# Moving the load and the transpose of an FFN bias to later places in a fused attention and FFN kernel

## The chip, the cores and the metric

One core of one Trainium2 chip. The metric is the device time of one execution in microseconds (us). All runs are on a single core; each kernel was run several times, and beside each kernel the kernel before was run on the same chip. The granted clock is the share of TensorE's full clock that the chip allowed, as the trace records it.

## The reference, cut to what matters

```python
# x: (1, 2048, 512), 32 heads of 128, 2048 cached keys and values, FFN width 1792
xn = layernorm(x)
q = (xn @ wq) split into 32 heads
o = softmax(q k^T / sqrt(128)) v
s = concat(o) @ wo
h = relu(xn @ w1 + b1) ** 2          # b1 has 1792 values: 14 rows of 128
g = silu(h @ w2 + b2)
out = x + s * g
```

The change touches only how b1 reaches its place. The kernel computes h with the FFN channels on the 128 partitions, so it needs b1 as 14 columns of 128. It loads it as 14 rows of 128 (a dense load), turns the rows into columns by a transpose on TensorE, and copies the result from PSUM to SBUF as 32-bit values.

## The kernel before

It is hand-scheduled: every instruction is emitted in a chosen order. A helper records what each instruction depends on and emits the waits. The beginning is written out by hand. The first head's keys come as rows in two halves and are transposed on TensorE. The query rows are normalised in four tiles of 128; each is transposed, projected for head 0 (`first_proj`) and head 1 (`second_proj`), and scores, exponentials and weighted sums (`gen_scores`, `gen_pv`) start as soon as a tile is there. After that a loop over 1024 steps keeps TensorE full (busy for 1206.00 of 1206.00 us between 16 and 1222 us in the profile below); projections and FFN matmuls are "fill jobs" between the steps.

```python
    # on GpSimd, after the memsets at the start
    tok_b1 = S.emit_dma(GP, partial(_dma, out=b1b[:], in_=B_b1.rearrange("(c p) -> c p", p=P)),
                        sl_b1)
    ...
    def bias_rows():
        t_b1[0] = E(PE, partial(_peT, out=psA[:, 1536:1600].bitcast(BF16)[:, 0:NFC], in_=b1b[:],
                                ident=ident[0:NFC, 0:NFC]), deps=[tok_b1, t_ident])

    def bias_copy():
        t_b1[0] = E(DV, partial(_copy, out=b1f[:],
                                in_=psA[:, 1536:1600].bitcast(BF16)[:, 0:NFC]), deps=[t_b1[0]])
    ...
    # gen_scores, first head: the scores are written to psA, where the bias columns lie for a moment
                      deps=[t_k0[b], t_q0[qt], t_exp[pi - 2] if pi >= 2 else t_b1[0]],
    ...
    # the beginning, in program order (cut)
    k0_copy(1)
    ln_rstd(0, 1, eng=DV)
    first_copy(0)
    first_proj(0)
    bias_rows()
    ln_scale(0, 1)
    first_evac(0)
    bias_copy()
    first_transpose(1)
    gen_scores(0)
    ln_bn(0, 2)
    gen_scores(1)
    ...
    first_evac(3)
    second_proj(3)
    second_evac()
    t_bankF[:] = [t_q0[3], tok_xT[0][3]]
    gen_pv(3)
    gen_scores(6)
```

The softmax here doesn't subtract the row's maximum and nothing guards it: scores larger than these inputs give would overflow.

## Time and profile before

| What | Value |
|---|---|
| Device time, median of 3 runs | 1237.77 us (1237.75 to 1237.85) |
| Execution that was profiled | 1238.05 us, span 1236.3 us |
| TensorE busy | 1231.7 us of the span |
| First scores start | 7.96 us |

The span is counted inside the execution; the device time is some 1.8 us longer. The profiled execution was 0.3 us slower than the timed ones. "PE" is TensorE's matmuls, "PEld" its weight loads, which run beside the matmuls: they are busy for 818.8 us and the matmuls for 1231.7 of a span of 1236.3 us, so they overlap. In a timeline line the first number is the start in us from the beginning of the span, the second the time covered, and the brackets give the idle time before and what ended it.

### The profile page before, as it was taken

What the parts mean: (1) busy time and instruction counts of PE and PEld (TensorE: products, weight loads), DVE (VectorE), ACT (ScalarE), POOL (GpSimd) and SP (SyncE); (2) the same over time, 40 slices, a digit from 0 to 9 for tenths busy, and PEclk for the clock granted to TensorE, in tenths of its full rate; (3) what the DMA queues carried; (4) which work ended last, traced back from release to release, by engine and by line L of the source; (5) the groups of instructions that cost most, each with busy time, mean ns of one, the idle gap of its engine ahead of it and who ended that gap; (6) DMA issues with size and microseconds to landing.
All of it is one profiled execution on the core that took longest, in us unless ns stands there. A gap on an engine that the chain in (4) does not pass through costs nothing.

```text
span 1236.3 us, 26934 instructions
## 1 busy us (share of the span) xinstructions
PE 1231.7 (100%) x11885; PEld 818.8 (66%) x11885; DVE 472.8 (38%) x953; ACT 1053.5 (85%) x1044; POOL 31.9 (3%) x73
## 2 busy tenths in 40 slices
PE   9999999999999999999999999999999999999999
PEld 7666666666666666666666666666666666666665
DVE  4453323244435332334444532333344333324333
ACT  7888888888888888888888888888888888888885
POOL 1010000000002000000000200000000000000000
PEclk9999999999999999999999999999999999999999
DMA  9999998777879897778778878787788789878771
GB/s 211 203 231 209 185 178 134 130 144 143 139 152 172 141 161 129 139 139 145 133 133 170 172 138 143 141 148 134 133 146 148 146 154 158 137 134 146 145 123 31
DMA packets 686868, 185.41 MB, mean 150 GB/s; under 512 B 673536, under 2 KB 685568, under 8 KB 686752
## 3 DMA queue, kind: packets, MB, share of 16 engines
q1 hardware_dynamic: 684656, 179.62, 80.4%
q0 software_dynamic: 1424, 3.81, 1.2%
q8 instruction: 94, 1.54, 0.6%
q10 hardware_dynamic: 672, 0.26, 0.1%
q14 instruction: 22, 0.18, 0.1%
HBM read 96.60 MB, written 2.10 MB: 80 GB/s over the span
## 4 chain that ended last, share of the span: by engine, by line
PE 99%; DMA 0%; DVE 0%; issue 0%; SPq 0%; DVEq 0%
PE psO L157 38%; PE psA L152 36%; PE psF L152 25%; DMA kT<-in_A_k_cache_dram 0%; PE psA L157 0%; DVE out_t L165 0%; PE psF L196 0%; DVE tmp_t L175 0%; PE psO L196 0%; PE psO L152 0%; DVE xnT L179 0%; SPq L208 0%; PE psA L196 0%; DVEq L119 0%
## 5 line engine op out<-in xcount | busy, mean ns | idle before, releaser
L161 ACT ACTIVATE pT<-psA 128x1024 bf16<-128x1024 f32 x1024 | 1043.5, 1023 | 163.5 <-PE psA L152 118.1
L157 PEld LDWEIGHTS psO<-v_sb,pT 128*128 128x128 bf16 x8192 | 547.7, 98 | 240.5 <-issue 12.5
L157 PE MATMUL psO<-v_sb,pT 128*128 128x129 bf16 x8192 | 631.6, 220 | 0.0
L152 PE MATMUL psA<-qt_sb,kT 128*128 128x512 bf16 x2032 | 604.8, 379 | 0.0
L179 DVE COPY o_un<-psO 128x258 f32<-128x258 f32 x256 | 97.4, 422 | 399.4 <-PE psO L157 398.7
L152 PE MATMUL psF<-xnT,wq_sb 128*128 128x512 bf16 (+1 forms) x520 | 168.9, 374 | 0.2 <-DVE xnT L179 0.2
L152 PE MATMUL psF<-wo_all,oT 128*128 128x512 bf16 x480 | 163.8, 379 | 0.0
L152 PEld LDWEIGHTS psA<-qt_sb,kT 128*128 128x128 bf16 x2032 | 156.9, 98 | 0.0
L179 DVE CAST qt_sb<-psF 128x512 bf16<-128x512 f32 (+1 forms) x130 | 88.0, 677 | 97.4 <-PE psF L152 97.4
L165 DVE TENSOR_TENSOR o_bf<-o_un,rden 128x512 bf16<-128x512 f32 x128 | 88.6, 692 | 4.7 <-DVE rden L183 0.3
L152 PEld LDWEIGHTS psF<-xnT,wq_sb 128*128 128x128 bf16 x520 | 50.2, 98 | 60.1 <-issue 0.3
L171 DVE TENSOR_SCALAR r_t<-psF,b1f 128x512 bf16<-128x512 f32 x56 | 42.0, 750 | 117.5 <-PE psF L152 117.5
L152 PEld LDWEIGHTS psF<-wo_all,oT 128*128 128x128 bf16 x480 | 46.9, 98 | 56.4
L152 PE MATMUL psF<-xnT,w_sb 128*128 128x512 bf16 x224 | 77.1, 379 | 0.0
L152 PE MATMUL psF<-w_sb,h2T 128*128 128x512 bf16 x224 | 74.2, 379 | 0.0
L152 PEld LDWEIGHTS psF<-xnT,w_sb 128*128 128x128 bf16 x224 | 21.9, 98 | 26.5
L152 PEld LDWEIGHTS psF<-w_sb,h2T 128*128 128x128 bf16 x224 | 21.9, 98 | 26.5
L165 DVE TENSOR_TENSOR z_t<-psF,b2bc 128x512 f32<-128x512 f32 x16 | 11.1, 692 | 67.2 <-PE psF L152 67.2
L165 DVE TENSOR_TENSOR acc<-psF,acc 128x512 f32<-128x512 f32 x28 | 19.3, 689 | 29.9 <-PE psF L152 29.9
L208 POOL DMA_DIRECT2D out_dram<-out_t x12 | 6.7, 554 | 891.0 <-DVE out_t L165 891.0
L165 DVE TENSOR_TENSOR h2T<-r_t 128x512 bf16<-128x512 bf16 x56 | 23.8, 425 | 1.9
L183 DVE RECIPROCAL rden<-o_un 128x4 f32<-128x4 f32 x128 | 22.9, 179 | 4.4
(47 smaller groups left out, 165.6 us busy)
## 6 DMA issues: line engine op xcount, KB each, us to landing
v_sb<-in_A_v_cache_dram SPq DMA_DIRECT2D x127, 512.0 KB, 4.7
wq_sb<-in_A_wq_dram SPq DMA_DIRECT2D x127, 128.0 KB, 3.1
wo_all<-in_A_wo_dram SPq DMA_DIRECT2D x4, 1024.0 KB, 6.7
w_sb<-in_B_w_dram SPq DMA_DIRECT2D x14, 256.0 KB, 4.3
oT<-o_bf SPq DMA_TRANSPOSE x128, 4.0
x_t<-in_A_x_dram POOLq DMA_DIRECT2D x16, 128.0 KB, 3.4
kT<-in_A_k_cache_dram SPq DMA_TRANSPOSE x127, 4.5
x_ln<-in_A_x_dram SPq DMA_DIRECT2D x15, 128.0 KB, 3.8
```

The costliest lines, as they stand in the source:

```text
L152: return e.matmul(out, lhsT, rhs, start=start, stop=stop)
L157: return e.matmul(out, lhsT, rhs, start=start, stop=stop, skip_group_check=True)
L161: return e.activation(out, in_, func, bias=bias, scale=scale)
L165: return e.tensor_tensor(out, in0, in1, op)
L171: return e.tensor_scalar(out, in0, scalar1=scalar1, scalar2=scalar2, op0=op0, op1=op1)
L179: return e.tensor_copy(out, in_)
L183: return e.reciprocal(out, in_)
L208: return e.dma_start(out, in_)
```

## The change

Its intent: take the small load out of the first microseconds, in which the keys arrive (the DMA engines are busy for 0.56 of the first 5 us), take the transpose off the way to the first scores, and free the first scores from a wait on the bias. The whole diff:

```diff
-    tok_b1 = S.emit_dma(GP, partial(_dma, out=b1b[:], in_=B_b1.rearrange("(c p) -> c p", p=P)),
-                        sl_b1)
-
@@ bias_rows, bias_copy
-        t_b1[0] = E(PE, partial(_peT, out=psA[:, 1536:1600].bitcast(BF16)[:, 0:NFC], in_=b1b[:],
-                                ident=ident[0:NFC, 0:NFC]), deps=[tok_b1, t_ident])
+        t_b1[0] = E(PE, partial(_peT, out=bankF(1)[:, 0:64].bitcast(BF16)[:, 0:NFC], in_=b1b[:],
+                                ident=ident[0:NFC, 0:NFC]), deps=[tok_b1, t_ident, tok_xT[0][TPB - 1]])
-                                in_=psA[:, 1536:1600].bitcast(BF16)[:, 0:NFC]), deps=[t_b1[0]])
+                                in_=bankF(1)[:, 0:64].bitcast(BF16)[:, 0:NFC]), deps=[t_b1[0]])
@@ gen_scores
-                      deps=[t_k0[b], t_q0[qt], t_exp[pi - 2] if pi >= 2 else t_b1[0]],
+                      deps=[t_k0[b], t_q0[qt], t_exp[pi - 2] if pi >= 2 else None],
@@ fill jobs
-    bank_no = [1]
+    bank_no = [0]
@@ the beginning
     ln_rstd(0, 1, eng=DV)
+    tok_b1 = S.emit_dma(GP, partial(_dma, out=b1b[:], in_=B_b1.rearrange("(c p) -> c p", p=P)),
+                        sl_b1)
     first_copy(0)
     first_proj(0)
-    bias_rows()
     ln_scale(0, 1)
     first_evac(0)
-    bias_copy()
@@
     second_proj(3)
     second_evac()
-    t_bankF[:] = [t_q0[3], tok_xT[0][3]]
+    bias_rows()
+    bias_copy()
+    t_bankF[:] = [t_q0[3], t_b1[0]]
     gen_pv(3)
```

## The prediction

> **What bounds the kernel now.** I read the page first: busy time by engine, then the granted clock, then the chain of waits. The columns of the engine line are busy time, share of the span and number of instructions.
>
> ```profile
> span 1236.3 us, 26934 instructions
> ...
> PE 1231.7 (100%) x11885; PEld 818.8 (66%) x11885; DVE 472.8 (38%) x953; ACT 1053.5 (85%) x1044; POOL 31.9 (3%) x73
> ...
> PEclk9999999999999999999999999999999999999999
> ...
> PE 99%; DMA 0%; DVE 0%; issue 0%; SPq 0%; DVEq 0%
> ```
>
> TensorE is busy in 1231.7 of 1236.3 us, its clock is full in all slices, and the chain that ended last is 99% TensorE work. Only 4.6 us of the span are not TensorE time. Then I asked for busy time by stretch (span of the stretch, busy time and instruction count per engine, granted clock), because an average doesn't say where those 4.6 us lie:
>
> ```profile
> 0.00:5.00 5.00, 4.02 (x36) 3.76 (x36) 1.22 (x4) 1.49 (x2) 2.14 (x13) 1.00 0.56 174
> 5.00:8.00 3.00, 2.48 (x31) 2.07 (x31) 2.44 (x9) 1.77 (x2) 1.02 (x2) 1.00 1.26 284
> 8.00:10.00 2.00, 2.00 (x34) 1.83 (x35) 1.55 (x6) 1.56 (x3) 0.73 (x2) 1.00 1.25 221
> 10.00:12.00 2.00, 1.93 (x35) 1.75 (x33) 1.15 (x5) 1.75 (x3) 0.27 (x2) 1.00 0.92 205
> ...
> 16.00:1222.00 1206.00, 1206.00 (x11604) 798.67 (x11602) 456.80 (x913) 1043.93 (x1034) 24.15 (x52) 1.00 0.83 150
> ```
>
> From 16 to 1222 us TensorE is busy in every recorded instant. The change touches nothing there, so this stretch can only start earlier or later as a whole; it cannot shrink. What the change is worth is decided in the first 16 us, and there by the moment at which TensorE's gap-free run begins. The chain of waits, in order of time, shows which pieces set that moment (start, duration, engine, target):
>
> ```profile
> 1.18 4.02 DMA kT<-in_A_k_cache_dram
> 5.20 0.05 issue
> 5.24 0.94 PE psO L196 x8
> 6.19 0.24 PE psF L196 x4
> 6.43 0.02 issue
> 6.45 0.43 DVE xnT L179
> 6.89 0.14 issue
> 7.02 0.38 PE psF L152 x4
> 7.41 0.11 PE psA L196
> 7.51 0.33 PE psF L196 x4
> 7.85 0.11 issue
> 7.96 1.05 PE psA L157 x16
> ```
>
> The first half of the keys has landed by 5.20 us; the bias transpose into psA is the single piece at 7.41 us, and the first scores start at 7.96. The timeline of the same moments gives the order on VectorE (start, duration, instruction):
>
> ```profile
> 7.44 0.29 DVE L179 CAST qt_sb<-psF 128x128 bf16<-128x128 f32 x1 [0.17 <-PE psF L152]
> ...
> 7.65 0.16 DVE L179 CAST b1f<-psA 128x14 f32<-128x14 bf16 x1
> 7.73 0.68 DVE L200 BATCH_NORM_STATS2 st_t<-x_ln 128x6 f32<-128x512 bf16 x1
> 7.93 0.91 PEld L157 LDWEIGHTS psA<-qt_sb,kT 128*128 128x128 bf16 x16 [0.26 <-issue]
> ```
>
> [...] my question is whether another engine lets TensorE wait, and the waits say no: the longest recorded TensorE wait other than at the start of the program is 0.2 us. [...] The queue view of the first 5.2 us shows how much: software_dynamic has 14 packets, 0.2% of the time of 16 engines. That is about 0.01 us per engine (0.002 x 5.2), and even that only if all of it lies before the keys. [...] The new place of the load lies beside a normalisation scale on VectorE[...]. The trace has one like case already: the output bias load was issued on GpSimd at 12.42 us with a scale at 12.50, and took 0.65 us against 0.73 us for the bias-row load at 1.98. [...]
>
> **The change part by part.**
>
> 1. The load of the 14 bias rows (3.5 KB) moves on GpSimd from behind the memsets (1.98 us) to behind the second reciprocal root, which ends at 6.27 + 0.55 = 6.82. GpSimd has nothing else to do before 8.91, so 0.73 us of issue ends near 7.6 and delays nothing. Taken out of the early traffic it frees the 0.01 us per DMA engine worked out above: the keys land at 5.19 instead of 5.20. I count 0.00 to 0.01 us.
>
> 2. The transpose leaves the place at 7.41 us. There it held TensorE for 0.11 us in front of the second tile's transposes. That is no gain of its own: those transposes would end near 7.75, but the scores behind them wait for the query columns anyway.
>
> 3. The scores no longer wait for the bias columns. The query cast ends at 7.44 + 0.29 = 7.73, the bias cast at 7.65 + 0.16 = 7.81; the first score weights load at 7.93, which is 0.12 us after the bias cast. The same handover from VectorE to TensorE took 0.12 us one step earlier (xnT copy ends 6.45 + 0.42 = 6.87, weight load 6.99). With the bias cast gone the query cast is the last to come: 7.73 + 0.12 = 7.85. Gain 0.08 us.
>
> 4. That gain has to be carried on, and each link of the next steps moves with it. VectorE's statistics start at 7.65 instead of 7.73 and so does everything behind them, including the third tile's root on GpSimd. The first exponential (8.60), which the first weighted sum at 9.68 waits for, follows the scores. So the 0.08 us reach 14.5 us whole.
>
> 5. The transpose comes back behind the fourth tile's second projection, near 14.4 us. TensorE is busy for 1.00 of 1.00 us between 14.5 and 15.5, so here it costs its full slot. In the dense stream eight weight load and matmul pairs with 128 or 129 columns take 0.45 us, 0.056 us a pair. This pair moves 14 columns but still loads weights; my estimate is 0.03 to 0.06 us, call it 0.05, and at worst the 0.11 us that the chain gave it before.
>
> 6. The cast to b1f comes back on VectorE behind the second head's query cast (14.76 + 0.69 = 15.45). Before, a copy of o_un started at 15.37, overlapping the end of the query cast; it now starts about 0.08 us later. The bank it frees is next written at 20.09 us; the second o_un copy, which also has to be done by then, starts only at 19.43. The first use of b1f is at 26.23. So this lies beside other work, 0 us.
>
> 7. The fill jobs begin with bank 0 instead of bank 1, so the first job (17.24 us) doesn't depend on the cast. The order of instructions differs on TensorE and VectorE in nothing but the moved pair; ACT and SP are the same. Both banks alternate as before, 0 us.
>
> Sum: -0.01 - 0.08 + 0.05 = -0.04 us. From 1237.77 that gives 1237.73, which I round to 1237.7 us. As a share of the time it is 0.003%.
>
> **The rivals.**
>
> A: the bias rows come late and TensorE, which runs in order, stands still at 14.4 us. The load took 4.6 us from issue to landing in the first 7 us, when the queues were crowded. From 6.84 that makes 11.4 us, 3.0 us before it is needed. The queues are as full there (DMA share 1.25 for 8 to 10 us), but even 7 us would do. If it did come late, every us over 7.5 would be added whole, since nothing downstream has slack; a landing of 10 us would give 1240.3.
>
> B: the early load really disturbed the keys by more than its packets[...]. Then the keys would land earlier by perhaps 0.1 to 0.2 us, with the chain behind them until VectorE's first scale (5.50 + 0.41 = 5.91) takes over as what the first transposes wait for: these start at 6.03, so no more than 0.05 to 0.1 us of it could be kept. Time 1237.6. Against it: most of its software-queue packets are served between 4.5 and 6.5 us, largely after the keys.
>
> C: the removed wait is replaced at once, because the half of the keys that the second group of scores needs, or the first exponential, has its own clock. ScalarE's two key copies end at 6.23 + 1.94 = 8.17 and the ninth score matmul runs at about 8.48, so 0.3 us of slack speak against it. In this case the gain is 0 and the added pair makes it 1237.8.
>
> D: the pair costs more in the dense stream than its slot, because a change of form breaks the overlap of weight loads. Then +0.1 us and 1237.8.
>
> **Range and chances.** B, C and D lie between 1237.6 and 1237.9. The before runs agree within 0.10 us (1237.75 to 1237.85), but its profiled run took 1238.05, so runs of the same kernel differ by some 0.3 us for other reasons. I put 1237.3 to 1238.1 as the range. A change of 2% would be 25 us, far more than the 4.6 us in which TensorE is not busy, so faster by over 2% is excluded by the profile; slower would take a long stall of rival A. Chances: 0.002 faster, 0.996 same, 0.002 slower.
>
> **What would show it.** In the changed kernel's timeline the first score weights should load at about 7.85 instead of 7.93 with the statistics on VectorE before them; the transpose of b1b should stand near 14.4 with no idle time in front; the bias load should be issued near 6.85 and land in 4 to 6 us; TensorE should be busy without a gap from 16 us on, and the span should be 1236.2 or 1236.3. An idle time of TensorE before the b1b transpose would prove A; keys landing before 5.1 would prove B; scores still at 7.93 would prove C; over 0.1 us between the second projection's last matmul and the third weighted sum would prove D. The whole prediction is wrong if TensorE's run from 16 to 1222 us changes its length.

The sum came to -0.04 us and so to 1237.73 us: -0.01 for the load, -0.08 for the wait, +0.05 for the transpose. The 0.01 us is my estimate from the queue view (which shows only "how much" of the engines' time went to the software queue: its 14 packets took 0.2% of the 16 engines' time in the first 5.2 us of `before`), and that the keys gain this time was assumed, not shown. The 0.05 us is an estimate from the 0.056 us of a full pair and the 0.11 us in the chain. The lower end of 0.03 us, rival B's 0.1 to 0.2 us and rival D's 0.1 us were guesses without a measurement behind them. The "like case" is all that is left of a worry that the load's issue on GpSimd would suffer from a scale on VectorE beside it. It did not here: in the changed kernel's trace the issue took 0.734 us at 6.53 us, with a scale on VectorE from 6.61 to 7.03, and in the profile before 0.727 us at 1.98 us, with VectorE idle.

## The result, and the profile after

The changed kernel took 1237.89 us in the median (1237.87 to 1238.15, 6 runs), the kernel before 1237.78 us (1237.74 to 1238.13, 6 runs). The ratio is 1.0001 with a 95% interval of 0.9988 to 1.0014: the same. (It is a ratio of means, so not quite that of the medians.) The medians lie 0.11 us apart, in the direction opposite to the predicted -0.04 us.

The page of the changed kernel:

```profile
span 1236.1 us, 26728 instructions
...
PE 1220.8 (99%) x11678; PEld 819.1 (66%) x11885; DVE 472.8 (38%) x953; ACT 1054.6 (85%) x1044; POOL 32.0 (3%) x73
```

TensorE seems 11 us less busy, but that is no effect: 11678 matmuls stand beside 11885 weight loads, so 207 matmul records are missing from this trace. Weight loads, which are complete, are busy for the same 819 us. And the span is 0.2 us *shorter* than in the profile before, while the timed runs are longer. The two profiles are of unequal executions, as the next lines show. The timeline of the changed kernel's beginning:

```profile
3.45 0.69 DVE L200 BATCH_NORM_STATS2 st_t<-x_ln 128x6 f32<-128x512 bf16 x1 [3.45 <-DMA x_ln<-in_A_x_dram]
...
7.14 0.29 DVE L179 CAST qt_sb<-psF 128x128 bf16<-128x128 f32 x1
7.35 0.68 DVE L200 BATCH_NORM_STATS2 st_t<-x_ln 128x6 f32<-128x512 bf16 x1
7.55 0.91 PEld L157 LDWEIGHTS psA<-qt_sb,kT 128*128 128x128 bf16 x16 [0.25 <-issue]
```

The first tile arrived at 3.45 us, where the profile before had its first statistics at 3.71, the keys' transposes start at 4.86 instead of 5.24, and the query cast at 7.14 instead of 7.44. So everything is 0.26 to 0.38 us early, 0.30 us at the query cast, before the bias transpose or the wait on it come into play. Counted from the query cast instead, the change is plain: the cast starts at 7.14 and the score weights load at 7.55, 0.41 us later; before it was 7.44 and 7.93, 0.49 us. That is the predicted gain of 0.08 us.

Where it goes is in the chain of waits around 14 us. (A piece of the chain lasts from the end of the piece before it to its own end.) Before:

```profile
14.50 0.22 PE psO L152 x4
14.72 0.45 PE psO L157 x8
15.17 0.89 PE psA L157 x16
```

After:

```profile
14.12 0.22 PE psO L152 x4
14.34 0.11 PE psF L196
14.45 0.56 PE psO L157 x8
15.01 0.89 PE psA L157 x16
```

At the second projection (psO, line 152) the changed kernel is 14.50 - 14.12 = 0.38 us ahead; that is 0.30 us of earlier arrival and the 0.08 us. At the scores behind (psA) it is 15.17 - 15.01 = 0.16 us ahead. Between them 0.22 us were lost: the transpose (psF, line 196) takes 0.11 us, and the eight matmuls behind it take 0.56 us where they took 0.45. The trace shows no wait for data there. The weight loads and matmuls of the changed kernel at this place:

```profile
13.90 0.27 PEld L152 LDWEIGHTS psO<-xnT,wq_sb 128*128 128x128 bf16 x4
13.95 0.39 PE L152 MATMUL psO<-xnT,wq_sb 128*128 128x128 bf16 x4
...
14.27 0.09 PEld L196 LDWEIGHTS psF<-ident,b1b 14*128 14x128 bf16 x1
14.27 0.18 PE L196 MATMUL psF<-ident,b1b 14*128 14x14 bf16 x1
14.38 0.46 PEld L157 LDWEIGHTS psO<-v_sb,pT 128*128 128x128 bf16 x8
...
14.38 0.63 PE L157 MATMUL psO<-v_sb,pT 128*128 128x129 bf16 x8
```

The same place in a second profile of the kernel before (`before_again`, below), where nothing stands between the two:

```profile
14.01 0.39 PE L152 MATMUL psO<-xnT,wq_sb 128*128 128x128 bf16 x4
14.18 0.49 PEld L157 LDWEIGHTS psO<-v_sb,pT 128*128 128x128 bf16 x8
...
14.23 0.62 PE L157 MATMUL psO<-v_sb,pT 128*128 128x129 bf16 x8
```

The projection's weight load starts at 13.90 and its first matmul at 13.95: a load runs ahead of its matmul by 0.05 us, under the matmul before it, as it does at 14.18 and 14.23 in the kernel before. The bias weight load and its matmul both start at 14.27, and the load behind and its matmul both start at 14.38. At both seams, the places where the bias pair meets its neighbours, the run-ahead is gone. Counted by starts, the whole loss lies in front of the eight matmuls: they start 0.43 us after the projection's first (13.95 to 14.38), where it was 0.22 us (14.01 to 14.23). They are not slower themselves (0.63 us in the timeline, 0.62 before): the chain counts by ends, and so books half of the loss to them.

### The profile page after: what moved, and what is told of

It reads as the page before. It is cut to its first block, busy times and chain, and to the rows that moved or that the text cites. A ratio compares the mean times of both kernels' runs of the same rounds, so it can differ in the third digit from the quotient of the medians.

```text
span 1236.1 us, 26728 instructions
## 1 busy us (share of the span) xinstructions
PE 1220.8 (99%) x11678; PEld 819.1 (66%) x11885; DVE 472.8 (38%) x953; ACT 1054.6 (85%) x1044; POOL 32.0 (3%) x73
## 4 chain that ended last, share of the span: by engine, by line
PE 98%; issue 1%; DVE 0%; DMA 0%; POOL 0%; DVEq 0%
PE psO L157 38%; PE psA L152 35%; PE psF L152 25%; PE psA L157 0%; DMA x_ln<-in_A_x_dram 0%; DVE out_t L165 0%; PE psF L196 0%; DVE tmp_t L175 0%; PE psO L152 0%; DVE xnT L179 0%; DVE st_t L200 0%; POOL rstd L165 0%; DVE xn_t L171 0%; DVE mv_t L204 0%; DVE ve_t L171 0%
## 5 line engine op out<-in xcount | busy, mean ns | idle before, releaser
L161 ACT ACTIVATE pT<-psA 128x1024 bf16<-128x1024 f32 x1024 | 1044.5, 1024 | 162.9 <-PE psA L152 117.6
L152 PE MATMUL psA<-qt_sb,kT 128*128 128x512 bf16 x1840 | 562.9, 379 | 10.1
L152 PE MATMUL psF<-xnT,wq_sb 128*128 128x512 bf16 (+1 forms) x508 | 165.7, 374 | 0.4 <-DVE xnT L179 0.2
```

The costliest lines, as they stand in the source:

```text
L152: return e.matmul(out, lhsT, rhs, start=start, stop=stop)
L161: return e.activation(out, in_, func, bias=bias, scale=scale)
```

## The experiments

Twelve experiments were run, on nine kernels with the two above. For each profiled execution I took its device time and the start of its first scores (the matmuls that write psA from qt_sb and kT), and subtracted:

| Run | Time, us | First scores, us | Rest, us | What stands behind the fourth projection |
|---|---|---|---|---|
| before, first profile | 1238.05 | 7.96 | 1230.09 | nothing |
| before_again | 1237.74 | 7.64 | 1230.10 | nothing |
| wait_only | 1237.76 | 7.64 | 1230.12 | nothing |
| wait_only_again | 1237.82 | 7.73 | 1230.09 | nothing |
| no_bias | 1237.74 | 7.66 | 1230.08 | nothing |
| changed, first profile | 1237.91 | 7.58 | 1230.33 | 14-row transpose |
| after_again | 1238.25 | 7.95 | 1230.30 | 14-row transpose |
| after_third | 1237.98 | 7.66 | 1230.32 | 14-row transpose |
| wait_early | 1237.92 | 7.58 | 1230.34 | 14-row transpose |
| early_load | 1238.10 | 7.76 | 1230.34 | 14-row transpose |
| full_rows | 1237.81 | 7.63 | 1230.18 | 128-row transpose |
| full_wait | 1237.68 | 7.52 | 1230.16 | 128-row transpose |
| x8 | 1238.28 | 7.78 | 1230.50 | eight 14-row transposes |
| late_load | 1241.57 | 10.59 | 1230.98 | nothing (half clock, see below) |

The rest is 1230.10 us on average without the transpose in the dense stream and 1230.33 with it, each within 0.04 us. So two numbers make up the time: when the first scores start, and what was put into the stream behind them. The table has one execution per row. The first scatters by up to 0.37 us within one kernel (7.58 to 7.95 in the three profiles of the changed kernel), which is more than anything the change does; the second does not scatter.

### The kernel before again, and the changed kernel again

No edit in either. The question: is the early arrival in the changed kernel's first profile its own doing?

> The kernel before, unchanged. Its first profile was taken of an execution of 1238.05 us, while its timed runs gave 1237.75 to 1237.85, so that profile may show a rarer, 0.3 us longer execution. Theory M (main): the early arrival of the first tile and keys in the changed kernel (first statistics at 3.45 us instead of 3.71, keys' transposes at 4.86 instead of 5.24) is not the change's doing; it differs from execution to execution. Then this profile, if its execution takes about 1237.8, should also show the statistics near 3.45 and the first scores near 7.66 (0.08 later than in the changed kernel). Rival B: taking the bias load out of the early traffic brings the keys earlier; then this profile shows again about 3.7 and 5.2, and first scores at 7.96. Time against before under both: ratio 1.0000, median 1237.8.

> The changed kernel, unchanged. Theory M: about 0.12 us above the kernel before (median 1237.9), because the first scores gain 0.08 us and the transpose in the dense stream costs 0.22 us. Rival N: the 0.11 us difference of the first medians is noise of the runs; then the medians here differ by less than 0.05 us or in the other direction.

Measured, before_again: 1237.75 us (1237.74 to 1237.86, 5 runs) beside 1237.80 for the same kernel in other runs. Its timeline:

```profile
3.43 0.69 DVE L200 BATCH_NORM_STATS2 st_t<-x_ln 128x6 f32<-128x512 bf16 x1 [3.43 <-DMA x_ln<-in_A_x_dram]
...
7.12 0.29 DVE L179 CAST qt_sb<-psF 128x128 bf16<-128x128 f32 x1
...
7.64 1.05 PE L157 MATMUL psA<-qt_sb,kT 128*128 128x128 bf16 x16
```

The kernel before, with its early load, has the first tile at 3.43 us and starts its keys' transposes at 4.79, even before the changed kernel's 4.86. So an early arrival comes without the change too; it differs from execution to execution. From query cast to first scores it takes 7.64 - 7.12 = 0.52 us, as in its first profile (7.96 - 7.44).

Measured, after_again: 1238.16 us (1237.91 to 1238.30), 0.36 us above before, three times the expected 0.12. Its profile, of an execution of 1238.25 us, shows why:

```profile
6.63 0.62 PE L196 MATMUL psO<-ident,kT 128*128 128x128 bf16 x8 [0.54 <-DMA kT<-in_A_k_cache_dram]
```

Here the second half of the keys came late; its transposes start at 6.63 instead of 5.95 us. They stand in front of the first projection in TensorE's order, so the query cast slips to 7.51 and the first scores to 7.95, which is again 0.44 us behind the cast. The rest of this execution, 1230.30 us, is that of the other profiles of the changed kernel.

### The wait alone

```diff
-                      deps=[t_k0[b], t_q0[qt], t_exp[pi - 2] if pi >= 2 else t_b1[0]],
+                      deps=[t_k0[b], t_q0[qt], t_exp[pi - 2] if pi >= 2 else t_b1[0] if pi else None],
```

This is an edit of the kernel before. The bias columns lie in psA from column 1536 on. The first group of scores writes columns 0 to 1023; the second writes 1024 to 2047, and still waits.

> The kernel before with one part of the change alone: the first group of scores no longer waits for the bias cast, only the second group does, which writes the PSUM banks in question. Load, transpose and cast stay at their old places. Theory M: first scores start 0.12 us after the query cast instead of 0.20 us, and the program ends 0.08 us earlier (median 1237.70). Rival C: another wait replaces it and the time stays at 1237.78.

> The best version so far with a right result, again: only the wait removed, everything else as before. Theory M: lowest runs 0.06 to 0.08 us below the lowest of before (1237.68 against 1237.74), the median below too unless the keys come late more often. First scores 1.43 us after the first xnT copy starts when the second half of the keys is early.

Measured: 1237.76 us (1237.68 to 1237.92) beside 1237.80, and in the second sample 1237.93 us (1237.82 to 1238.18, 4 runs) beside 1237.82. In the first trace:

```profile
7.20 0.29 DVE L179 CAST qt_sb<-psF 128x128 bf16<-128x128 f32 x1 [0.23 <-PE psF L152]
...
7.64 1.05 PE L157 MATMUL psA<-qt_sb,kT 128*128 128x128 bf16 x16
```

From cast to scores 0.44 us instead of 0.52, and 0.44 again in the second sample (7.29 and 7.73). Rival C, another wait in its place, falls: the gain of 0.08 us at the first scores is real. It is too small to show in medians: the lowest run is 0.06 us below the lowest of before in one sample and 0.09 us above it in the other, so the expected order of the lowest runs held once and failed once. In both profiled executions the second half of the keys came late (transposes at 6.32 and 6.41 us, 5.93 in before_again). The expected 1.43 us from the first xnT copy to the scores was missed for this reason in both (6.10 to 7.64, and 6.22 to 7.73).

### Neither load, transpose nor cast

```diff
-    t_b1 = [None]
+    t_b1 = [E(GP, partial(_memset, out=b1f[:], val=0.0))]
...
-    tok_b1 = S.emit_dma(...)
-    bias_rows()
-    bias_copy()
-    t_bankF[:] = [t_q0[3], t_b1[0]]
+    t_bankF[:] = [t_q0[3], tok_xT[0][TPB - 1]]
```

This is an edit of the changed kernel, with a bias of zeros. The comparison with the reference still called the output correct, so it doesn't resolve this bias; no conclusion on b1's correctness rests on that check.

> The changed kernel without the bias load, transpose and cast; the bias columns are zeros (a wrong result on purpose). Theory M: what the late transpose costs comes back, 0.22 us below the changed kernel and 0.08 to 0.1 us below the kernel before: 1237.67. Rival P (my prediction's sum): the transpose costs only 0.05 us, so 1237.84 if the changed kernel is at 1237.89. Rival N (noise): no order among the three.

Measured: 1237.64 us (1237.58 to 1238.05) beside 1237.80. The rest falls from 1230.33 to 1230.08 us, to the value of the kernel before. The late transpose with its surroundings costs 0.25 us by this run, 0.23 us by the averages of the table. Rival P, my own 0.05 us, falls.

### Why 0.22 us: the wait, or the shape?

Two kernels, both edits of the changed one. In the first the wait for the load moves to the projection before, so that the transpose carries no new wait:

```diff
-                          deps=[t_wqfill[1], tok_xT[0][i], t_k0[1]], inc=(c == NDC - 1))
+                          deps=[t_wqfill[1], tok_xT[0][i], t_k0[1], tok_b1 if i == TPB - 1 else None],
+                          inc=(c == NDC - 1))
```

In the second the bias rows lie in a tile of 128 rows, zeros below, and the transpose is a full one:

```diff
-    b1b = sb("b1b", [NFC, P], BF16)
+    b1b = sb("b1b", [P, P], BF16)
+    t_b1z = E(GP, partial(_memset, out=b1b[:], val=0.0))
...
-        ... out=bankF(1)[:, 0:64].bitcast(BF16)[:, 0:NFC], in_=b1b[:], ident=ident[0:NFC, 0:NFC] ...
+        ... out=bankF(1)[:, 0:64].bitcast(BF16)[:, 0:P], in_=b1b[:], ident=ident[:] ...
-    ... out=b1b[:], in_=B_b1... , sl_b1)
+    ... out=b1b[0:NFC, :], in_=B_b1... , sl_b1, deps=[t_b1z])
```

> The changed kernel with the wait for the bias load put on the second projection of the fourth tile, so that the bias transpose itself waits for nothing new. Theory W: the semaphore wait in front of the transpose keeps its weight load from running ahead, and that makes up about half of its 0.22 us; then the transpose and the weighted sum behind it take 0.11 us less and the time is about 1237.78. Theory R: the partial shape (14 rows) is what breaks the overlap with the neighbours; then nothing changes, 1237.9.

> The changed kernel with the bias rows in a 128-row tile, zeros below row 14, so that the transpose is a full 128 by 128 one like those of the activations. The load waits for a memset of that tile. Theory R: a full-row weight load runs ahead under the matmuls before it, and the following pair's load under it; the cost falls from 0.22 us to the 0.056 us of a pair in the stream, time about 1237.73. Theory W: still 0.2 us, time 1237.9.

Measured, wait_early: 1237.96 us (1237.89 to 1238.62) beside 1237.85; its chain has the same 0.11 us for the transpose and 0.56 us for the eight matmuls behind, rest 1230.34. Theory W falls.

Measured, full_rows: 1237.81 us (1237.67 to 1238.06) beside 1237.85, rest 1230.18. Its chain and its timeline:

```profile
14.39 0.06 PE psF L196
14.45 0.45 PE psO L157 x8
```

```profile
14.18 0.10 PEld L196 LDWEIGHTS psF<-ident,b1b 128*128 128x128 bf16 x1
...
14.23 0.49 PEld L157 LDWEIGHTS psO<-v_sb,pT 128*128 128x128 bf16 x8
14.29 0.62 PE L157 MATMUL psO<-v_sb,pT 128*128 128x129 bf16 x8
```

A transpose that moves nine times the columns costs about a quarter here: 0.06 us with its seams instead of 0.22. The weight loads run ahead again (14.18 for the transpose at 14.23, 14.23 for a matmul at 14.29). A full load takes 0.10 us here and a pair comes every 0.056 us (0.45 us for eight), so the loads overlap the matmuls. Theory R stands: the shape sets the cost. It is not separated whether the 14 rows of weights or the 14 moving columns matter, since this kernel changes both.

The second sample, beside the changed kernel's third (the expectation speaks of another chip, but it fell on the same one as the first sample):

> The full-row transpose again, on another chip and beside the changed kernel in the same call. Theory R: its lowest runs lie 0.16 us below those of the changed kernel (0.22 less 0.056), so near 1237.71, and its trace shows again 0.06 us at the transpose and 0.45 us for the eight matmuls behind it.

Measured: 1238.10 us in the median of 4 runs (1237.68 to 1238.30) beside 1237.82. The lowest run is where it was expected, 0.15 us below the lowest of the changed kernel; the median is a miss, and two of four executions took 1238.3. The profiled execution took 1237.68, and its trace has 0.06 and 0.45 us and a rest of 1230.16. The slower executions have no profile, so what slowed them is not shown.

### Eight transposes in a row

```diff
-    bias_rows()
+    for _ in range(8):
+        bias_rows()
```

> The changed kernel with the bias transpose done eight times in a row at its new place (same result). Both theories give the price of a repeated pair. If each pair of 14 rows costs a full unoverlapped 0.11 us, the time rises by 7 x 0.11 = 0.77 us to 1238.66; if only the first and last of such a run pay and those between run at 0.056 us or less, it rises by at most 0.39 us to 1238.3.

Measured: 1238.28 us (1237.98 to 1238.64) beside 1237.85, rest 1230.50, so 0.17 us above one transpose. The chain:

```profile
14.54 0.28 PE psF L196 x8
14.82 0.56 PE psO L157 x8
```

Eight take 0.28 us where one takes 0.11: (0.28 - 0.11) / 7 = 0.024 us for each further one. Behind them the same 0.56 us. So a further 14-row transpose is cheap (0.024 us); the rest of the 0.22 us comes with the change of form between its neighbours and it, once going in and once coming out. The eight weight loads of this run, too, follow each other faster than one of them lasts (eight in 0.26 us, 0.09 us for a single one): among themselves they overlap.

### The late load without the late transpose

The kernel before with only the load moved:

```diff
-    tok_b1 = S.emit_dma(...)          # at the start
     ln_rstd(0, 1, eng=DV)
+    tok_b1 = S.emit_dma(...)
     first_copy(0)
```

> The kernel before with only the load moved to its new place, and transpose and cast left at their old ones. Rival A of the prediction is made true here on purpose: TensorE runs in order and waits for the bias rows at about 7.1 us, which land at 6.5 + 3.8 = 10.3 us in the changed kernel's trace. Expected: an idle time of TensorE of about 3 us in front of the b1b transpose, and a time 3 to 3.5 us above before, 1240.8 to 1241.3. If the program gives a part of it back later it is less.

Measured: 1242.81 us (1241.57 to 1242.99) beside 1237.85, ratio 1.0038 (1.0024 to 1.0052). The profiled execution is the fastest, 1241.57. The wait in its timeline, and its busy times by stretch (the column before the last two is the granted clock):

```profile
10.04 0.19 PE L196 MATMUL psA<-ident,b1b 14*128 14x14 bf16 x1 [2.86 <-DMA b1b<-in_B_b_dram]
```

```profile
7.20:10.00 2.80, 0.00 (x0) 0.00 (x0) 0.29 (x1) 0.63 (x1) 0.00 (x0) 0.89 1.33 231
10.00:12.00 2.00, 1.96 (x19) 1.89 (x20) 1.18 (x4) 0.34 (x1) 0.37 (x2) 0.50 1.08 243
```

TensorE idles 2.86 us for the rows, as expected; the time, even of the fastest execution, is above the expected 1240.8 to 1241.3. What I had not expected comes after: the clock is granted at 0.50 from 10 to 12 us, and the first 16 score matmuls take 1.89 us in the timeline where they take 1.05 at full clock. These 0.84 us are nearly all of the 0.88 us by which the rest is too long (1230.98 - 1230.10). The mean granted clock is 0.89 from 7.2 to 10 us and 0.80 from 12 to 14 us. If it was 0.50 while it was low and 1.00 otherwise, these means place the low clock from about 9.4 to 12.8 us (my estimate: 0.11 x 2.8 / 0.5 = 0.6 us before 10, 0.20 x 2.0 / 0.5 = 0.8 us after 12): it began some 2.2 us after TensorE's last work (7.18 us) and lasted some 3.4 us. This is one trace, and no run here has a shorter gap of this kind to compare. Together, 10.59 - 7.64 = 2.95 us of later start and 0.88 us make the 3.83 us between this execution and before_again's. So load and transpose had to move together. The four other executions took 1242.15 to 1242.99, up to 1.4 us more; their mean granted clock is 0.997 to 0.998, against 0.999 in the profiled one, which would fit more of the low clock. When and why is not shown, as they have no profile.

### The late transpose without the late load, and the changed kernel a third time

early_load is the changed kernel with the load back at the start (the inverse of the diff above).

> The changed kernel with only the load put back to its old, early place; transpose and cast stay behind the fourth tile's projection. It separates the load's place from the rest. Theory M: the load's place does nothing beyond the scatter of arrivals; the time is that of the changed kernel, about 0.13 us above before in the lowest runs (1237.87), with the 0.22 us at the transpose in the trace. Rival B: the early load disturbs the keys, so this kernel is slower than the changed one in its lowest runs and its keys land later.

> The changed kernel a third time, beside the two early-load kernels of this call. Its four slow runs of five in the second sample came with a late second half of the keys (second key transposes at 6.63 us). Theory M: that lateness is scatter, so most runs here lie again at 1237.87 to 1237.95, and the lowest is 0.13 us above the lowest of before. Rival L: the late load itself makes the second half late; then again most runs lie above 1238.1 while those of the kernel before do not.

Measured beside 1237.82 for before: early_load 1238.10 us (1237.92 to 1238.32), rest 1230.34; after_third 1237.90 us (1237.83 to 1238.23), rest 1230.32. In early_load the first half of the keys was transposed from 4.80 us and the second from 6.27; in after_third from 4.63 and 6.33. Over all profiles the first half was transposed from 4.79 to 5.34 us with the early load (five profiles) and from 4.63 to 5.29 us with the late one (eight), the second half from 5.93 to 6.41 and from 5.95 to 6.63. The ranges lie over each other, so no effect of the load's place is shown. But the means for the first half, 5.06 and 4.88 us, differ in rival B's direction, and so few profiles don't exclude its 0.1 to 0.2 us. Four of five runs of early_load lie above 1238.05 and one of five of after_third, which speaks a little for rival B and against rival L; but over all its samples the changed kernel has 6 of 16 there (four of them in after_again) and the kernel before 6 of 30. With so few runs and the scatter that the kernel before shows (1237.73 to 1238.33 on this chip) I don't take it as shown. Both traces have the 0.11 and 0.56 us.

### No version beats both

By the two-number model the version of wait_only is the best with a right result (rest as before, first scores 0.08 us earlier), then full_rows, whose gain of 0.08 us is eaten by 0.07 us. No run separates either from the kernel before: 0.08 us is less than a quarter of the scatter of arrivals.

## Why the prediction was right or wrong, point by point

The time was in the range and "same" was right; the sign of the small difference was wrong. The range of 0.8 us was wider than every part of the sum, so that the time fell into it says nothing for the parts; the traces have to judge them. Over all samples, 16 runs of the changed kernel have a median of 1237.91 us and a lowest of 1237.83, 30 runs of the kernel before 1237.78 and 1237.73. The intervals cover zero, but the sum of the parts that the traces show, -0.08 + 0.23 = +0.15 us, fits both differences (0.13 and 0.10 us) within the scatter.

- The bound (TensorE gap-free from 16 us on, so only the beginning counts): held. The rest in the table, constant to 0.04 us for the same stream, shows it, and the 11602 weight loads between 16 and 1222 us are busy for 798.67 us in the profile before and 799.11 us in the one after.
- Steps 1 and 2 (the load's place, the transpose's old place): nothing to be seen, as worked out. The load was issued at 6.53 and landed 3.8 us later, at 10.3 us, 4 us before it is needed; rival A didn't occur, and late_load shows what it would have cost.
- Step 3 and 4 (0.08 us at the first scores, carried on whole): right. The cast-to-scores time is 0.52 us in both profiles of before and 0.44 us in all three of the changed kernel, and the 0.08 us are still there at the second projection.
- **Step 5 is the term that failed.** "This pair moves 14 columns but still loads weights; my estimate is 0.03 to 0.06 us, call it 0.05, and at worst the 0.11 us" took the price of a pair in the stream and the place in it for granted. It cost 0.22 to 0.23 us: 0.11 at the transpose and 0.11 at its follower as the chain counts, where both lost the run-ahead of the weight load; full_rows, which keeps the run-ahead, cost 0.06. Rival D named this mechanism and allowed it 0.1 us more than the estimated slot of 0.05 us and a time of 1237.8; it was 0.17 us more. Its sign, over 0.1 us between the projection and the weighted sum, was just met (0.11 us in the chain).
- Steps 6 and 7 (VectorE's cast, the banks): right. The o_un copy started right behind the cast (14.99 and 15.06 us) and nobody waited.
- Rival B looked right in the first pair of profiles: the sign it had named, keys landing before 5.1 us, was there. But before_again, with the early load, shows the same, so the sign proves nothing; a small mean effect stays open (see early_load). What the prediction held against B was weaker than it reads: of the load's 32 packets 14 had been served by 5.2 us. I had read the keys' landing at 5.20 us in the profile of before as its normal course, although that execution was 0.3 us slower than the timed ones. In before_again they had landed by 4.79.

## What to carry to other kernels

The transpose in its gap cost next to nothing (from cast to scores 0.44 us with it in wait_only, 0.43 us without it in no_bias); moved into a gap-free stream it cost its slot and the seams on both sides, 0.22 us together. The seams were the larger part, most of the 0.22 us, and a full-size transpose cost a quarter of the small one (0.06 us). Look for the wait that a change removes and remove that alone: the dependency of the first scores could be dropped without moving anything. And when two single profiles are compared, check first whether both executions have the same time; a quantity such as "time less first scores" that doesn't scatter shows effects that medians cannot.
